# A first batch led through the weights' conversion by ties: the order of three streams on VectorE

## The chip, the cores and the metric

The kernel runs on one core of a Trainium2 chip. The metric is device time in microseconds, the median of several executions, compared with executions of the kernel before on the same chip. An execution counts as fast, or as slow where it lies over 1.5% above the fastest of the same kernel. The span of a profile is some 1.7 us shorter than the time of the same execution.

## The reference

Four batches of attention with a polynomial feature map, followed by a mixing of tokens with phases:

```python
# q, k, v: (4 batches, 4 heads, 1088 tokens, 32), S1, S2: (8, 32)
def phi(x):
    a = einsum('rd,bhsd->bhsr', S1, x)
    b = einsum('rd,bhsd->bhsr', S2, x)
    return einsum('bhsi,bhsj->bhsij', a, b).reshape(..., 64)
q_p, k_p = phi(q), phi(k)
kv  = einsum('bhsf,bhsd->bhfd', k_p, v)
num = einsum('bhsf,bhfd->bhsd', q_p, kv)
den = einsum('bhsf,bhf->bhs', q_p, k_p.sum(axis=2))[..., None] + 1e-6
x = num / den                                # to (4, 1088, 128)
theta = x @ w_theta
zr, zi = x * cos(theta), x * sin(theta)
y = einsum('ts,bsd->btd', w_tok_r, zr) + einsum('ts,bsd->btd', w_tok_i, zi)
u = x + y
out = u + maximum(u @ w_ch, 0)
```

The weights `w_tok_r` and `w_tok_i` (1088 x 1088 each) come as 64-bit floats, which the kernel turns into 32-bit ones.

## The kernel before

Three streams share VectorE (DVE) and ScalarE (ACT): the 34 pieces of weights, batch 0, and batch 1. The builder places instructions on each engine by rank; `level` sets the rank, and the ranks are, best first: first (batch 0), weights, out, attention (batches 1 to 3), mixing.

```python
def load_f32(dst, src):                     # one piece of weights, 128 x 544
    st = stg.tile([P, PIECE], I64, tag="st", ...)             # 4 buffers
    nc.sync.dma_start(st, src)
    step = stg.tile([P, PIECE, 2], I16, tag="step", bufs=2)
    A.activation(dst, ...); A.activation(step[:, :, 1] ...); A.activation(step[:, :, 0] ...)
    ts(x, x, 3, ALU.logical_shift_left)     # the two VectorE passes of a piece
    tt(V, x, x, step ..., ALU.add)

def keys_slices(b):                         # ... largest key, power of two ipk
    for h in range(H):
        A.activation(kx[:, :, h], kn[:, :, h], AF.Copy, scale=ipk[:, b, 0, h:h + 1])
    ks = work.tile([P, 3, NC * P], F16, tag="ksl", bufs=1)    # a buffer of its own
    big = work.tile([P, NC * P], F32, tag="r", bufs=1)
    # ... five VectorE passes of 128 x 1152: the keys in three f16 slices
# query_slices(b): likewise, into q0, q1, q2 of their own
# matrices(b): key sums, then a few dozen small dependent steps to the feature matrix mv[b]
# keys_values(b), features(b), denominators(b), queries(b, g): to x and z, three groups of tokens

def attention(b):
    features(b)
    denominators(b)
    for g in range(NG):
        queries(b, g)

with level("first"):
    # ... loads, S1 and S2 in tiles of their own
    query_slices(0); matrices(0); keys_values(0, spare); attention(0)
with level("attention"):
    keys(1); attention(1); keys(2)
mixing(0, True)                             # 102 matmuls: 17 rows of weights, 3 groups, 2 halves each
with level("attention"):
    attention(2); keys(3)
mixing(1, False)
# ... attention(3), mixing(2, False), mixing(3, False)
```

A mixing matmul shows in the trace as two half-matmuls, and counts below ("102") are of these: 17 rows x 3 groups x 2.

## Time and profile before

| before | |
|---|---|
| time | 358.36 us (358.15 to 359.53, 3 runs; a fourth came with the result) |
| span of the profile | 357.9 us |
| mv of batch 0 complete | 77.6 us |
| last weights pass on VectorE ends | 117.4 us |
| key slices of batch 1 complete | 120.2 us |
| mv of batch 1 complete | 154.5 us |
| first z of batch 1 (its start) | 188.8 us |

### The profile page before, as it was taken

The numbers are of one execution on the slowest core, as the hardware profiler recorded it, in microseconds if no ns is written. First come the engines' busy times: TensorE is split into PE (matmuls) and PEld (weight loads), VectorE is DVE, ScalarE is ACT, GpSimd is POOL, SyncE is SP. The second block draws the span as 40 slices with busy tenths as digits, with TensorE's granted clock in tenths as the row PEclk, the third lists the DMA queues.
The fourth block names the chain that finished last, engine by engine and source line by source line (L and its number), as shares of the span: only waits on it lengthen the run. The fifth ranks groups of instructions, "written<-read, shape, count | busy, mean of one in ns | idle before, by whom it ended". The sixth has DMA issues, their size and how long they took to land.

```text
span 357.9 us, 4021 instructions
## 1 busy us (share of the span) xinstructions
PE 274.9 (77%) x1355; PEld 192.1 (54%) x1355; DVE 250.4 (70%) x713; ACT 153.8 (43%) x313; POOL 0.7 (0%) x6
## 2 busy tenths in 40 slices
PE   0406680145327999999689999996999999999994
PEld 0304480023226676776357777674777766776562
DVE  4898886985996699559948794896589569542111
ACT  0799729997958442061134413312335131332000
POOL 0000000000000000000000000000000000000000
PEclk9999955556555899999969999997899999999998
DMA  7668447883720012020010122000000000000010
GB/s 289 214 229 269 153 145 243 293 304 108 238 59 4 2 65 69 0 67 3 22 40 2 65 66 70 21 22 20 0 0 3 0 9 15 22 20 0 0 44 18
DMA packets 11604, 28.78 MB, mean 80 GB/s; under 512 B 1216, under 2 KB 5568, under 8 KB 11584
## 3 DMA queue, kind: packets, MB, share of 16 engines
q1 hardware_dynamic: 11376, 28.51, 24.3%
q8 instruction: 10, 0.16, 0.2%
q14 instruction: 10, 0.08, 0.1%
q10 hardware_dynamic: 208, 0.02, 0.0%
HBM read 26.30 MB, written 2.23 MB: 80 GB/s over the span
## 4 chain that ended last, share of the span: by engine, by line
PE 69%; DVE 17%; ACT 8%; DMA 3%; issue 1%; ACTq 0%
PE y L566 36%; PE w L519 4%; PE acc L398 3%; ACT step L135 3%; PE w L539 2%; PE y L576 2%; PE y L398 2%; PE w L446 2%; ACT step L136 2%; DVE wT L93 2%; PE w L513 2%; PE w L388 2%; DMA s_t_st<-s_t 2%; PE acc L306 2%; PE w L447 2%; PE w L534 1%
## 5 line engine op out<-in xcount | busy, mean ns | idle before, releaser
L566 PE MATMUL y<-wT,zst 128*128 128x384 f32 (+1 forms) x384 | 134.8, 481 | 1.4 <-DVE zst L93 1.4
L566 PEld LDWEIGHTS y<-wT,zst 128*128 128x128 f32 x384 | 68.1, 193 | 30.6 <-DVE zst L93 2.3
L585 ACT COPY ot<-y 128x384 f32<-128x384 f32 (+2 forms) x16 | 6.0, 398 | 62.1 <-PE y L580 62.1
L135 ACT ACTIVATE step<-st 128x544 f16<-128x544 f32 (+1 forms) x35 | 27.8, 795 | 4.3 <-DVE wT L93 4.2
L93 DVE CUSTOM_DVE_ANT_0 wT<-wT,step 128x1088 uint16<-128x1088 uint16 x34 | 24.4, 718 | 5.8 <-ACT step L136 5.8
L519 PEld LDWEIGHTS w<-kvbd,qpT 128*128 128x128 f32 x144 | 21.6, 213 | 11.3 <-ACT qpT L517 10.4
L136 ACT ACTIVATE step<-st 128x544 int16<-128x544 uint32 (+1 forms) x35 | 27.4, 784 | 0.0
L519 PE MATMUL w<-kvbd,qpT 128*128 128x64 f32 x144 | 23.4, 297 | 3.2 <-ACT qpT L517 3.1
L134 ACT ACTIVATE wT<-st 128x544 f32<-128x544 f32 x34 | 22.9, 685 | 2.3 <-DMA st<-w_tok 2.2
L517 ACT COPY qpT<-w 128x256 f32<-128x256 f32 x36 | 12.9, 367 | 24.6 <-PE w L513 24.5
L513 PE MATMUL w<-ident,qp 128*128 128x128 f32 x72 | 14.6, 304 | 7.7 <-DVE qp L93 7.6
L93 DVE TENSOR_TENSOR uT<-xT,y 128x384 f32<-128x384 f32 (+1 forms) x12 | 6.3, 529 | 19.2 <-PE y L566 19.1
L97 DVE TENSOR_SCALAR tn<-w 128x384 f32<-128x384 f32 x12 | 6.7, 557 | 17.8 <-PE w L539 17.8
L536 ACT COPY xT<-w 128x384 f32<-128x384 f32 x12 | 5.7, 475 | 29.8 <-PE w L534 29.8
L449 ACT COPY lv<-w 128x384 f32<-128x384 f32 x36 | 14.9, 504 | 8.3 <-PE w L448 8.2
L513 PEld LDWEIGHTS w<-ident,qp 128*128 128x128 f32 x72 | 10.1, 170 | 9.8 <-ACT wT L134 8.1
L97 DVE TENSOR_SCALAR wT<-wT 128x544 int32<-128x544 int32 x34 | 14.6, 435 | 0.0
L446 PE MATMUL w<-mv,q 128*128 128x384 f16 x36 | 13.4, 372 | 0.8 <-DVE mv L93 0.8
L398 PEld LDWEIGHTS acc<-ld_v,kp 128*128 128x128 f32 x108 | 13.0, 192 | 1.5
L539 PEld LDWEIGHTS w<-w,xT 128*128 128x128 f32 x72 | 10.6, 215 | 5.2 <-ACT xT L536 4.5
L404 ACT COPY kvbd<-acc 64x64 f32<-64x64 f32 x6 | 1.2, 206 | 27.6 <-PE acc L398 27.6
L100 DVE SCALAR_TENSOR_TENSOR fl<-lv 128x864 f32<-128x864 f32 x4 | 4.2, 1054 | 12.3 <-ACT lv L449 12.3
(230 smaller groups left out, 523.5 us busy)
## 6 DMA issues: line engine op xcount, KB each, us to landing
st<-w_tok SPq DMA_DIRECT2D x34, 544.0 KB, 4.6
ld_k<-k_l SPq DMA_DIRECT2D x4, 576.0 KB, 4.0
ld_q<-q_l SPq DMA_DIRECT2D x4, 576.0 KB, 4.4
ld_v<-v_l SPq DMA_DIRECT2D x4, 576.0 KB, 3.8
out<-ot SPq DMA_DIRECT2D x8, 192.0 KB, 2.1
out<-ot SPq DMA_DIRECT2D x4, 128.0 KB, 1.8
st<-w_sq SPq DMA_DIRECT2D x1, 256.0 KB, 4.6
out<-ot SPq DMA_DIRECT2D x4, 32.0 KB, 1.8
```

The lines of the kernel that those rows point to most:

```text
L93: eng.tensor_tensor(out=o, in0=a, in1=b, op=op)
L97: V.tensor_scalar(out=o, in0=a, scalar1=s1, scalar2=s2, op0=op0, **kw)
L134: A.activation(dst, hi.bitcast(F32), AF.Copy, scale=2.0**-112)
L135: A.activation(step[:, :, 1].bitcast(F16), hi.bitcast(F32), AF.Copy, scale=2.0**-60)
L136: A.activation(step[:, :, 0], lo.bitcast(U32), AF.Copy, scale=2.0**-29)
L398: nc.tensor.matmul(kv[:, n], kp[:, i * H + 2 * n:i * H + 2 * n + 2].rearrange("p h i j -> p (h i j)"), vn[:, c, 2 * n:2 * n + 2].rearrange ...
L446: nc.tensor.matmul(lp, q0, flat[:, 0:4 * W], start=True, stop=False, skip_group_check=True)
L449: A.copy(lv[:, :, :, c].rearrange("p l t n -> p (l t) n"), lp.rearrange("p (x n) -> p x n", n=HR))
L513: nc.tensor.transpose(tr[:, n * P:(n + 1) * P], qp[:, i * H + 2 * n:i * H + 2 * n + 2].rearrange("p h i j -> p (h i j)"), ident)
L519: nc.tensor.matmul(num[:, i * P + n * 2 * D:i * P + (n + 1) * 2 * D], qpT[:, n], kvbd[b][:, n], start=True, stop=True)
L539: nc.tensor.matmul(th[:, i * P:(i + 1) * P], xT[:, i * P:(i + 1) * P], w2[:, 0], start=True, stop=True)
L566: nc.tensor.matmul(yp[:, :t1 - t0], z, wT[:, i, t0:t1], start=(i == 0), stop=(i == NK - 1))
```

## The change

The intent is to bring batch 0 to its mixing early. Its parts:

- **Ties.** The VectorE passes of each piece of weights are queued behind a chosen instruction of batch 0's chain, a few pieces per place. Seven pieces instead of 23 then lie ahead of mv(0).
- **Split.** Batch 0's features, denominators and queries go group by group (three groups of tokens).
- **Hold.** Batch 1's VectorE work is queued behind batch 0's first group.
- **Row order.** Rows of weights are loaded and mixed in the order of the groups (real and imaginary row of a chunk side by side), so mixing can start on the first group.
- **S1 and S2** in one tile of 128 x 48.
- To make room, the key and the query slices share one buffer ("sl"); batch 0's z gets a tile of its own; three step buffers instead of two.

```diff
+    order = [j * NF + i for i in range(NF) for j in range(2)] + [NK - 1]
...
-        for i in range(NK):
+        for i in order:
             for n in range(0, S, PIECE):
                 load_f32(wT[:, i, n:n + PIECE], w_tok[i][:, n:n + PIECE])   # notes both passes in `rows`
...
-        ks = work.tile([P, 3, NC * P], F16, tag="ksl", name="ksl", bufs=1)
+        ks = work.tile([P, 3, NC * P], F16, tag="sl", name="ksl", bufs=1)
...
-        sl = [work.tile([P, NC * P], F16, tag=f"q{i}", name=f"q{i}", bufs=1) for i in range(3)]
+        sl = work.tile([P, 3, NC * P], F16, tag="sl", name="qsl", bufs=1)
...
-        query_slices(0)
-        matrices(0)
-        keys_values(0, spare)
-        attention(0)
+        keys_features(0)
+        matrices(0)                      # gate(1) at three places inside
+        query_slices(0)
+        gates.extend([tiles["ready", 0]] * 3)
+        with tc.issue_after(tiles["ready", 0]):
+            for g in range(NG):
+                features(0, g * GC, (g + 1) * GC)
+                if g == 0:
+                    keys_values(0, spare)
+                denominators(0, g * GC, (g + 1) * GC)
+                gate(3)
+                mixed(0, g, numerator(0, g))
+                gate(4)
+                if g == 0:
+                    behind = last_on_dve()
+        gate(2 * NK)
+        for i, ins in enumerate(rows):   # order on VectorE alone, no wait
+            tc.add_manual_dep(ins, gates[i // 2].name, ...)
     with level("attention"):
-        keys(1)
+        with tc.issue_after(behind):
+            load(1, "kqv")
+            keys_powers(1)
+            query_powers(1)
+            keys(1)
         attention(1)
         keys(2)
```

(`gate(n)` puts the last VectorE instruction so far n times on the list of places; cut here: S1 and S2, the split of functions, buffers.)

## The prediction

> **What bounds the kernel now.** I read the busy shares and slices of the page first, then each engine's busy time in stretches cut at four events, then the chain that ended last, the costs by form, and the order of time of each engine in the first 190 us.
>
> ```profile
> PE 274.9 (77%) x1355; PEld 192.1 (54%) x1355; DVE 250.4 (70%) x713; ACT 153.8 (43%) x313; POOL 0.7 (0%) x6
> ...
> PE   0406680145327999999689999996999999999994
> ...
> DVE  4898886985996699559948794896589569542111
> ACT  0799729997958442061134413312335131332000
> ...
> PEclk9999955556555899999969999997899999999998
> ```
>
> TensorE is nearly full from the 13th slice on, but in the first 12 (to about 115 us) it is busy for less than half and from the 6th has a halved clock, while VectorE and ScalarE turn the 34 pieces of 64-bit weights into floats and carry the first batch through its small steps. The four stretches are: keys of batch 0 in until its feature matrix mv is ready (77.3); until the first mixing matmul of batch 0 (115.9); until the first of batch 1 (189.7); the rest.
>
> ```profile
> 4.80:77.30 72.50, 26.50 (x125) 20.34 (x126) 60.36 (x223) 55.95 (x98) 0.00 (x0) 0.78 0.70 237
> 77.30:115.90 38.60, 19.34 (x77) 13.75 (x76) 30.17 (x67) 30.84 (x56) 0.00 (x0) 0.54 0.38 121
> 115.90:189.70 73.80, 69.03 (x357) 47.64 (x358) 56.13 (x141) 22.05 (x51) 0.00 (x0) 0.93 0.11 33
> 189.70:357.90 168.20, 159.64 (x798) 110.29 (x796) 102.26 (x267) 44.97 (x110) 0.00 (x0) 0.97 0.07 21
> ```
>
> (After the stretch and its length: PE, PE weight load, DVE, ACT, POOL busy, clock, DMA share, GB/s.) The fourth stretch is 95% TensorE: its 168.2 us stay unless that work changes. In the third TensorE is full too, but with filler: the mixing of batch 0 is there while batch 1 creeps forward. Its chain of waits shows that the stretch ends on batch 1 and not on TensorE:
>
> ```profile
> 173.20 0.56 DVE uT L100
> ...
> 177.16 0.76 DVE r L97
> ...
> 180.62 1.22 DVE ksl L100
> ...
> 189.72 1.35 PE y L566 x4
> ```
>
> The last mixing matmuls of batch 0 end near 172.5; then VectorE carries the chain (denominators of batch 1, slices of batch 2), and TensorE can mix again at 189.7. So the time is: start of batch 1's mixing, plus 168.
>
> **What the Trainium skill says.** (1) "TensorE: Matmul & The Clock Gate", Part 1, says that the array runs at half clock until it has been busy for some 3.4 us and falls back when idle. The trace agrees: the stretch 77.3 to 115.9 was granted 0.54, the later ones 0.93 and 0.97, and four half-matmuls of the mixing take 2.92 us at 115.9 but 1.35 us at 189.7. (2) The same page, "Architectural detail", says that VectorE and ScalarE take their queue strictly first in, first out. So a weights pass that waits for ScalarE stops everything behind it; the trace has VectorE idle 2.52 us before a weights pass at 56.3, with batch 0's next small copy behind it. (3) "VectorE: DVE Perf Modes", the errata section, gives every VectorE operation a fixed cost beside its length (151 cycles for fp32 tensor_tensor). Here 128x288 takes 0.45 us and 128x1152 1.36, which fit that to 0.01 us, so an operation cut in three pays the fixed cost three times.
>
> **The change part by part.**
>
> *Weights.* The same 34 pieces, the same passes:
>
> ```profile
> L135 ACT ACTIVATE step<-st 128x544 f16<-128x544 f32 x34 | 27.3, 804 | 4.3 <-DVE wT L93 4.2
> L136 ACT ACTIVATE step<-st 128x544 int16<-128x544 uint32 x34 | 27.0, 793 | 0.0
> L93 DVE CUSTOM_DVE_ANT_0 wT<-wT,step 128x1088 uint16<-128x1088 uint16 x34 | 24.4, 718 | 5.8 <-ACT step L136 5.8
> L134 ACT ACTIVATE wT<-st 128x544 f32<-128x544 f32 x34 | 22.9, 685 | 2.3 <-DMA st<-w_tok 2.2
> L97 DVE TENSOR_SCALAR wT<-wT 128x544 int32<-128x544 int32 x34 | 14.6, 435 | 0.0
> ```
>
> Issued back to back, a piece takes 0.64+0.35 = 1.0 us on VectorE and 1.9 on ScalarE (starts at 60.87, 62.79, 64.68). What is new is their place. By the built order only 7 pieces lie before mv(0) instead of 23; 20 lie between there and the last z of batch 0, and 7 behind it.
>
> *S1 and S2 in one tile* take away some 15 VectorE instructions of 0.1 to 0.2 us each: about 2 us, on the first path. Splitting batch 0's denominators into three adds two more sets of about 24 instructions with the same elements in all: 48 fixed costs near 0.1 us, +5 us of VectorE. (The built order has 755 VectorE instructions against 715.)
>
> *Stage A, to mv(0).* I summed the start-to-start times of VectorE instructions in the new order, from the operation on the keys at 4.8 to the last writing of mv: 35.6 us, where the old stretch had 60.4. Following the waits by hand (keys' slices start near 14 instead of 18.5, the 18 key-sum matmuls run about 25.5 to 30.5, then the small cuts, 0.2 us for each dependent one, and four round trips to TensorE) adds about 11 us: mv(0) near 51, 26 us earlier.
>
> *Stage B, to the end of batch 0's mixing.* Behind that stand 58.8 us of VectorE: 27 pieces 26.6, denominators about 20, kp and qp 5.2, x, tn, tt, z 7.2. ScalarE has about 24 pieces less what three step buffers hold ready, 45 us, and 13 of batch 0: 58. Two equal loads that wait for each other do not run at 100%: at the 83% of the first old stretch (60.4 of 72.5) the 58.8 become 71, so about 122. TensorE must also do 17 mixing matmuls after the last z: 17 x 0.65 at full clock = 11 us from about 115. Both say about 122 to 126, against 115.9 for the *start* of this mixing before. The mixing (102 half-matmuls, about 33 us) is thus gone from the later path, but the front ends later.
>
> *Stage C, batch 1 to its first mixing.* The order puts batch 1's key slices behind the last weights and beside batch 0's output. VectorE has 45.3 us there; before it had 56.1 in 73.8 us (76%). At 76% this is 60 us. Followed by hand with nothing left to fill the waits (slices 8, key sums 4.5, to mv(1) 24, features 7, denominators, qp and slices of batch 2 20, x to z 7) it is about 68 to 70.
>
> *Stage D* stays 168.2.
>
> Sum by shares: 122 + 2 + 60 + 168 = 352. Sum by steps: 125 + 68 + 168 = 361. The share method lets waits be as well filled as they were, the step method puts them all end to end, which overlaps less than engines do; gates placed with this much care also suggest that someone found them useful on the chip, which favours the lower one. I take 354.
>
> **The rivals.**
>
> *1. The front is what counts, and TensorE's 33 us come off the end.* If batch 0 leaves the front by 112 (ScalarE's bare sum, 51 + 58, plus a last pass) and batch 1's small steps run fast because TensorE's queue is empty (60 us), mixing 1 starts near 172: 340. For it: TensorE was 94% busy in the third stretch, so small matmuls of batch 1 stood in a queue. Against: VectorE had 17.7 us idle there, yet the stretch is a chain of some 150 dependent VectorE steps, whose length TensorE hardly sets.
>
> *2. Batch 1 becomes bare.* What was taken off TensorE was filler, so the gap moves from 40-115 us to about 125-190, at half clock: features of a batch take 0.72 us a group at half clock (77.6, 78.3, 79.0) against 0.37 at full (157.55, 157.92). Then C is 70 or more and the time 360 to 368. For it: the order has no mixing between batch 0's end and batch 1's first z. Against: C also loses batch 0's x, tn, tt and z.
>
> *3. DMA becomes the bound.* 24 pieces of 544 KB in about 70 us are less than the 304 GB/s reached at 60 to 80 us. I hold this unlikely.
>
> **Range and chances.** Stage B may be off by 7 us either way, C by 6, A by 4, and D by 3: together about 10. The middle of the two sums less the lean gives 354, and 8 in 10 from 343 to 365. Two per cent are at 351.2 and 365.5. So 0.38 for faster, 0.50 within, 0.12 slower.
>
> **What would show it.** Right: the last piece of mv(0) near 51; the last weights pass near 122 (before 116.7); nearly all of batch 0's mixing between 76 and 126; a stretch of 60 to 68 us behind it in which TensorE is less than half busy at a low clock and VectorE's waits are for TensorE; then about 168 us as before. Wrong: weights ending before 112 (my stage B loses too much to waits); batch 1's first mixing less than 55 us behind batch 0's last (then rival 1, and TensorE's queue was what slowed batch 1); or a fourth stretch that differs from 168 by over 4 us, because mixing in the new order of rows starts better or because the later batches come apart.

## More of the kernel before

A line holds start, length, engine, source line, operation, output<-input, and in brackets the idle time before it with what ended it.

```profile
77.74 0.15 DVE L97 TENSOR_SCALAR ipk<-pw 128x4 f32<-128x4 f32 x1
...
108.14 0.44 DVE L97 TENSOR_SCALAR wT<-wT 128x544 int32<-128x544 int32 x1
108.49 0.75 DVE L97 TENSOR_SCALAR ksl<-kx 128x1152 f16<-128x1152 f32 x1
...
110.00 0.71 DVE L93 CUSTOM_DVE_ANT_0 wT<-wT,step 128x1088 uint16<-128x1088 uint16 x1
...
116.67 0.71 DVE L93 CUSTOM_DVE_ANT_0 wT<-wT,step 128x1088 uint16<-128x1088 uint16 x1
117.30 0.75 DVE L97 TENSOR_SCALAR r<-kx 128x1152 f32<-128x1152 f32 x1
118.09 0.76 DVE L97 TENSOR_SCALAR ksl<-r 128x1152 f16<-128x1152 f32 x1
118.88 1.36 DVE L100 SCALAR_TENSOR_TENSOR ksl<-kx,ksl 128x1152 f16<-128x1152 f32 x1
```

The scale of batch 1's keys (ipk) is there at 77.9. Batch 1's key slices (ksl) begin at 108.5, between passes of the weights (wT) and before batch 0's first z; they are done 3 us behind the last weights pass.

## The result, and the profile after

| | before | after |
|---|---|---|
| time, median of 4 | 358.94 us (358.15 to 359.90) | 378.11 us (376.12 to 379.49) |
| span of the profile | 357.9 | 375.4 |
| mv(0) complete | 77.6 | 54.5 |
| last weights pass ends | 117.4 | 132.0 |
| key slices of batch 1 complete | 120.2 | 139.2 |
| mv(1) complete | 154.5 | 172.0 |
| first z of batch 1 | 188.8 | 205.8 |

The changed kernel is slower: the ratio is 1.053, with a 95% interval from 1.047 to 1.059. A ratio here is the mean time of one kernel's fast runs over that of the other's of the same rounds, so not quite the ratio of the medians quoted.

The page of the changed kernel (busy times; busy tenths of 40 slices; chain that ended last):

```profile
PE 287.1 (76%) x1355; PEld 200.3 (53%) x1355; DVE 257.2 (69%) x753; ACT 155.2 (41%) x311; POOL 0.7 (0%) x6
...
PE   1655039659699967088147999998899999999994
...
PEclk9999555568989989555656999999699999999999
...
PE 58%; DVE 25%; ACT 12%; issue 2%; DMA 2%; SPq 0%; ACTq 0%; DVEq 0%
```

TensorE (PE) is busier in the first 14 slices on the whole than before, as intended. But a hole has opened in slices 15 to 22, some 132 to 206 us, with a low clock. In the chain VectorE has 25%, where the page of before has 17. Cut at the same four events as in the prediction (columns as there):

```profile
4.80:54.40 49.60, 19.64 (x85) 13.84 (x85) 40.59 (x160) 30.64 (x54) 0.00 (x0) 0.81 0.58 198
54.40:132.00 77.60, 64.00 (x259) 44.36 (x259) 61.62 (x177) 60.49 (x106) 0.00 (x0) 0.79 0.52 166
132.00:206.50 74.50, 42.48 (x208) 31.17 (x208) 50.24 (x130) 19.08 (x43) 0.00 (x0) 0.66 0.08 24
206.50:375.40 168.90, 160.60 (x805) 110.83 (x803) 103.08 (x270) 45.02 (x110) 0.00 (x0) 0.97 0.07 21
```

The fourth stretch is unchanged (168.9 for 168.2). So nearly the whole loss of 17.5 us in the span is that batch 1's first z comes 17 us later. The order of time on ScalarE and VectorE around the last weights says what stands before it:

```profile
130.50 0.79 ACT L147 ACTIVATE step<-st 128x544 int16<-128x544 uint32 x1
131.16 1.78 ACT L304 ACTIVATE kx<-ld_k,ipk 128x288 f32<-128x288 f32 x4
```

```profile
118.71 0.16 DVE L108 TENSOR_SCALAR ipk<-pw 128x4 f32<-128x4 f32 x1
...
131.31 0.72 DVE L104 CUSTOM_DVE_ANT_0 wT<-wT,step 128x1088 uint16<-128x1088 uint16 x1 [0.83 <-ACT step L147]
131.96 0.55 DVE L104 TENSOR_TENSOR uT<-xT,y 128x384 f32<-128x384 f32 x1
132.97 0.76 DVE L108 TENSOR_SCALAR ksl<-kx 128x1152 f16<-128x1152 f32 x1 [0.47 <-ACT kx L304]
...
137.82 1.35 DVE L111 SCALAR_TENSOR_TENSOR ksl<-kx,ksl 128x1152 f16<-128x1152 f32 x1
```

The scale of batch 1's keys (ipk) is there at 118.9, 41 us later than before: the hold keeps batch 1 back until batch 0's first z at 81.6, and then its first VectorE passes stand behind others of better rank. Its four scalings on ScalarE (kx) come 12 us later, behind the last of the weights' passes (step, 130.50), and the slices on VectorE behind those. Before, the slices began at 108.5. In the stretch behind it, VectorE's waits are nearly all for TensorE or for ScalarE's copies of its results (us in total, times, longest):

```profile
DVE fl L111 <- ACT lv L486: 4.2, 1, 4.2
DVE tn L108 <- PE w L583: 3.1, 1, 3.1
DVE pw L230 <- PE acc L227: 3.0, 1, 3.0
DVE cm L104 <- PE acc L327: 2.0, 1, 2.0
DVE kp L104 <- PE acc L431: 1.9, 1, 1.9
```

### The profile page after: what moved, and what is told of

Its sections match the earlier page's. It is cut to its first block, busy times and chain, and to the rows that moved or that the text cites. A ratio compares the mean times of both kernels' runs of the same rounds, so it can differ in the third digit from the quotient of the medians.

```text
span 375.4 us, 4081 instructions
## 1 busy us (share of the span) xinstructions
PE 287.1 (76%) x1355; PEld 200.3 (53%) x1355; DVE 257.2 (69%) x753; ACT 155.2 (41%) x311; POOL 0.7 (0%) x6
## 3 DMA queue, kind: packets, MB, share of 16 engines
q1 hardware_dynamic: 11584, 28.53, 23.4%
## 4 chain that ended last, share of the span: by engine, by line
PE 58%; DVE 25%; ACT 12%; issue 2%; DMA 2%; SPq 0%; ACTq 0%; DVEq 0%
PE y L610 25%; PE acc L431 4%; PE w L554 4%; ACT step L147 3%; PE w L583 3%; PE w L413 2%; ACT step L146 2%; PE y L431 2%; PE w L548 2%; ACT wT L145 2%; DVE lv L104 2%; ACT lv L486 2%; DVE qp L104 2%; PE w L483 2%; PE y L620 2%
## 5 line engine op out<-in xcount | busy, mean ns | idle before, releaser
L610 PE MATMUL y<-wT,zst 128*128 128x384 f32 (+1 forms) x288 | 100.8, 475 | 0.0
L610 PEld LDWEIGHTS y<-wT,zst 128*128 128x128 f32 x288 | 49.8, 190 | 19.3 <-issue 0.7
L610 PE MATMUL y<-wT,z 128*128 128x384 f32 (+1 forms) x120 | 45.8, 514 | 7.3 <-DVE z L104 6.0
L610 PEld LDWEIGHTS y<-wT,z 128*128 128x128 f32 x120 | 23.4, 208 | 21.3 <-DVE z L104 7.0
L145 ACT ACTIVATE wT<-st 128x544 f32<-128x544 f32 x34 | 23.4, 695 | 9.6 <-DMA st<-w_tok 9.6
L431 PEld LDWEIGHTS acc<-ld_v,kp 128*128 128x128 f32 x108 | 17.2, 238 | 2.5 <-DVE ipn L382 0.3
L483 PE MATMUL w<-mv,qsl 128*128 128x384 f16 x36 | 14.4, 400 | 5.2 <-DVE mv L104 4.2
L431 PE MATMUL acc<-ld_v,kp 128*128 128x64 f32 x108 | 16.9, 319 | 0.3 <-DVE ipn L382 0.3
L548 PEld LDWEIGHTS w<-ident,qp 128*128 128x128 f32 x72 | 10.6, 177 | 10.5 <-issue 9.7
L325 PE MATMUL acc<-ksl 128*128 128x384 f16 x27 | 9.9, 389 | 7.4 <-DVE ksl L111 7.4
L349 PE MATMUL acc<-sz,cz 128*128 128x32 f16 (+3 forms) x16 | 2.8, 182 | 16.3 <-DVE cz L108 16.3
```

Source lines behind the costliest of these rows:

```text
L145: A.activation(dst, hi.bitcast(F32), AF.Copy, scale=2.0**-112)
L431: nc.tensor.matmul(kv[:, n], kp[:, i * H + 2 * n:i * H + 2 * n + 2].rearrange("p h i j -> p (h i j)"), vn[:, c, 2 * n:2 * n + 2].rearrange ...
L483: nc.tensor.matmul(lp, q0, m[:, 0:4 * W], start=True, stop=False, skip_group_check=True)
L548: nc.tensor.transpose(tr[:, n * P:(n + 1) * P], qp[:, i * H + 2 * n:i * H + 2 * n + 2].rearrange("p h i j -> p (h i j)"), ident)
L610: nc.tensor.matmul(yp[:, :t1 - t0], z, wT[:, i, t0:t1], start=(n == 0), stop=(n == NK - 1))
```

## The experiments

Two theories stood at the start. **Queue:** ties, hold and split put batch 1's chain behind the weights, so it starts late. **Bareness:** what was taken off TensorE was filler, so batch 1's chain runs at a low clock and gets longer. A rival to both was the prediction's own: less work on TensorE in that stretch should be a gain. (In the expectations, G stands for the ties and H for the hold, the two parts of Queue; C for the clock, which is Bareness; S for the split.) Eighteen kernels were run, all of them correct but one that is wrong on purpose; each edit is against the changed kernel unless it says otherwise. One table holds what they gave (events in us, from the profiled run; the last column is the time left behind the first z of batch 1):

| run | time, us | ratio to before | last weights | key slices (1) | mv(1) | first z(1) | rest |
|---|---|---|---|---|---|---|---|
| before | 358.9 | 1 | 117.4 | 120.2 | 154.5 | 188.8 | 169.2 |
| after | 378.1 | 1.053 | 132.0 | 139.2 | 172.0 | 205.8 | 169.6 |
| no_gates | 370.4 | 1.027 | 100.7 | 130.5 | 169.1 | 201.5 | 168.2 |
| no_hold | 374.2 | 1.041 | 138.3 | 125.4 | 169.3 | 203.8 | 168.6 |
| no_gates_no_hold | 367.6 | 1.024 | 98.8 | 131.0 | 164.7 | 195.4 | 169.6 |
| filler | 371.4 | 1.031 | 132.7 | 140.2 | 169.6 | 201.9 | 168.4 |
| before_mix0_one_row | 368.4 | 1.024 | 117.4 | 121.8 | 163.9 | 198.0 | 169.9 |
| both_unsplit | 354.2 | 0.985 | 102.7 | 112.7 | 146.9 | 182.9 | 169.5 |
| both_mix_late (slow profile) | 365.8 | 1.010 | 98.7 | 128.3 | 161.3 | 197.0 | 169.8 |
| mix_late | 369.8 | 1.029 | 130.6 | 135.7 | 165.5 | 198.8 | 168.3 |
| unsplit_only | 375.8 | 1.047 | 128.5 | 135.3 | 170.1 | 204.5 | 169.6 |
| both_unsplit_mix_late | 351.1 | 0.980 | 104.1 | 114.1 | 146.6 | 182.2 | 167.1 |
| before_s_merged | 360.2 | 1.004 | 118.9 | 122.1 | 154.7 | 188.6 | 168.8 |
| unsplit_no_gates | 359.8 | 1.003 | 101.8 | 124.5 | 153.5 | 188.8 | 168.5 |
| ties_at_mv0 | 376.2 | 1.051 | 120.8 | 132.5 | 169.9 | 204.3 | 169.8 |
| unsplit_no_hold | 348.4 | 0.973 | 135.1 | 85.7 | 135.5 | 177.7 | 169.5 |
| before_row_order | 360.6 | 1.007 | 115.4 | 118.3 | 152.9 | 187.4 | 171.3 |
| before_mix_late | 362.8 | 1.014 | 117.3 | 121.7 | 158.2 | 191.8 | 169.7 |
| unsplit_keys1_first (slow profile) | 354.4 | 0.986 | 141.7 | 112.0 | 158.5 | 191.9 | 169.6 |
| keys1_first (slow profile) | 360.7 | 1.001 | 145.1 | 115.8 | 163.0 | 194.9 | 169.7 |

(A slow profile is of a run over 1.5% above that kernel's fastest; its events are then some us late, and only the ratio, which leaves such runs out, is compared.) The rest is 167 to 171 us in all of them: **the span is the first z of batch 1 plus about 169**, and the end of the weights says nothing of it. The last weights come at 98.8 in a run of 367.6 and at 135.1 in one of 348.4. The runs were made in rounds on several chips, where the kernel before took 358.0 to 359.8 us; so a difference of some 2 us between times of different rounds is not to be read, and the ratios are the better measure.

### no_gates: without the ties

```diff
-        for i, ins in enumerate(rows):
-            tc.add_manual_dep(ins, gates[i // 2].name, ...)
```

> The changed kernel without the ties of the weights' VectorE passes to chosen places; all else as changed. By the built order some 20 pieces of weights then lie ahead of mv(0) again (7 in the changed kernel), and batch 1's key slices come ahead of batch 0's last x instead of behind the last weights. Theory G (the ties made it slow: they pile weights, denominators and the groups into one stretch that ends at 132 instead of 117): mv(0) near 68, last weights pass near 118 to 122, first mixing matmul of batch 1 near 190, time 358 to 364. Rival B (bareness: whatever the order of weights, batch 1's chain has no filler and is as long): the last weights end earlier, but the chain to batch 1's first mixing stays 74 us or more behind it only where batch 1 starts late; time 368 to 378.

370.4 (one run of four slow; the fast ones mean 369.4), interval of the ratio 1.021 to 1.033: 7.7 us of the 19 come back, between the two theories. mv(0) was at 66.9, the last weights at 100.7. But batch 1's key slices still came only at 130.5, though no weights were left to stand before them: the first began at 118.43, right behind batch 0's last feature matmul (118.08), for a reason that the next run shows. The ties are one hand in the loss and not the whole.

### no_hold: without the hold

```diff
-        with tc.issue_after(behind):
+        if True:
```

> The changed kernel without the order edges that hold batch 1 behind batch 0's first group; ties of the weights stay. The built order puts batch 1's key slices among the last groups of batch 0 instead of behind the last weights. Theory H (holding batch 1 made stage C long): stage C, from the last weights pass to batch 1's first mixing matmul, falls from 74.5 to about 62, the last weights move from 132 to about 139, time 371 to 374. Theory G (the ties): 376 to 380, since the same VectorE work only changes places.

374.2, ratio 1.038 to 1.043: 4 us, at the upper edge of theory H. The lines below (ScalarE, then TensorE, then VectorE) show why so little:

```profile
60.08 0.54 ACT L304 ACTIVATE kx<-ld_k,ipk 128x288 f32<-128x288 f32 x1
```

```profile
103.56 0.25 PE L485 MATMUL w<-mv,qsl 128*128 128x192 f16 x1
```

```profile
103.84 0.76 DVE L108 TENSOR_SCALAR ksl<-kx 128x1152 f16<-128x1152 f32 x1 [0.52 <-PE w L485]
...
117.53 0.70 DVE L108 TENSOR_SCALAR ksl<-r 128x1152 f16<-128x1152 f32 x1
124.09 1.35 DVE L111 SCALAR_TENSOR_TENSOR ksl<-kx,ksl 128x1152 f16<-128x1152 f32 x1
```

The scaled keys are ready at 60.6, yet the first slice is taken at 103.8, when TensorE's L485 has ended. That is batch 0's last feature matmul, in the third group: it reads the query slices, and these share the buffer "sl" with the key slices. So the slices wait 43 us with their input ready; in one piece (unsplit_no_hold below) batch 0 is done with the buffer at 64.5, and they wait 8. Batch 1's slices nevertheless begin 5 us before those of the kernel before, and are spread over 22 us; from their end to mv(1) it takes 44 us where it took 34, while the weights go on beside them to 138.3. So an early start alone is not enough. VectorE sits idle for only 0.52 us before it, because the builder had put other work in front; so a list of waits doesn't show this dependence at its size.

### no_gates_no_hold: both away

The two edits above together.

> The changed kernel without ties and without the hold of batch 1; what stays is the split of batch 0 into groups, S1 and S2 in one tile, the order of rows. If ties and hold together are the whole loss, this is 352 to 359 (the before time less some us for S1 and S2). If the split of batch 0 into three groups and the early mixing are the loss themselves, 368 to 378.

367.6, just under the second range. Ties and hold together are 10.5 of the 19 us. The scaled keys are ready at 103.5, and again the first slice follows batch 0's last feature matmul:

```profile
118.60 0.25 PE L485 MATMUL w<-mv,qsl 128*128 128x192 f16 x1
```

```profile
118.96 0.76 DVE L108 TENSOR_SCALAR ksl<-kx 128x1152 f16<-128x1152 f32 x1 [0.59 <-ACT tn L589]
```

### filler: useless matmuls in the hole

```diff
     mixing(0, True)
+    with level("mixing"):
+        mix_sums(0, range(NG), [psum(ps_y, "y") for _ in range(NG)])
```

> The changed kernel with batch 0's 102 mixing matmuls issued a second time, into PSUM that nobody reads, at the lowest priority: the built order puts them where TensorE stood idle in stage C (from the last weights to batch 1's first mixing), and leaves VectorE's order as it was. It adds 33 us of TensorE at full clock and does nothing useful. Theory C (half clock: with nothing to do TensorE drops to half clock and every round trip of batch 1's chain grows): clock in stage C over 0.85, the 24 kv matmuls go from 8.0 to about 4 us, the features from 7.4 to about 4, stage C falls from 74.5 to 64 to 68, time 367 to 372. Rival B (the chain of dependent VectorE steps sets stage C, TensorE's clock hardly): 375 to 380. Rival Q (small matmuls of batch 1 queue behind mixing matmuls): slower, 380 to 390.

The kernel does 102 half-matmuls more, to no use, and is **6.7 us faster**: 371.4, ratio 1.026 to 1.035, in the range of theory C. VectorE's order hardly differs. First the changed kernel, then the filler run: the stretch 150 to 189, and the 36 kv matmuls of batch 1.

```profile
150.00:189.00 39.00, 19.31 (x86) 14.92 (x86) 23.75 (x84) 6.87 (x16) 0.00 (x0) 0.57 0.07 25
```

```profile
150.00:189.00 39.00, 37.47 (x184) 24.99 (x183) 29.06 (x91) 7.20 (x19) 0.00 (x0) 1.00 0.08 28
```

```profile
L431 PE MATMUL acc<-ld_v,kp 128*128 128x64 f32 x36 | 8.0, 420 | 0.3 <-DVE ipn L382 0.3
```

```profile
L431 PE MATMUL acc<-ld_v,kp 128*128 128x64 f32 x36 | 4.2, 272 | 0.0
```

The clock goes from 0.57 to 1.00, the kv matmuls from 8.0 to 4.2 us, and the stretch from the last weights to batch 1's first mixing from 74.5 to 69.8, less than the 64 to 68 expected. So bareness costs some 5 us of the 19 here, and is not the whole either.

### before_mix0_one_row: useful filler taken away

On the kernel before, batch 0 mixes one row of weights instead of 17; batch 0's output is wrong.

```diff
-        for i in range(NK):
+        for i in (range(NK) if b else (NK - 1,)):
-                nc.tensor.matmul(..., start=(i == 0), stop=(i == NK - 1))
+                nc.tensor.matmul(..., start=(i == (0 if b else NK - 1)), stop=(i == NK - 1))
```

> The kernel before with the mixing of batch 0 cut from 17 rows of weights to one (96 of 102 half-matmuls gone; batch 0's output is wrong on purpose). Theory C (what TensorE does in that stretch is filler, and keeps its clock up): 31 us of TensorE go, the clock between 132 and 189 falls from near 1.0 to 0.5 to 0.6, and the time does not fall: 357 to 364. The prediction's rival 1 (TensorE's 33 us come off the end): 325 to 345. Theory between (the chain of VectorE sets it, clock of no account): 354 to 358.

With 96 half-matmuls less, some 31 us of TensorE, the kernel before gets **9 us slower**: 368.4, ratio 1.021 to 1.027, beyond even the range of theory C. First the kernel before, then this run, from 132 to 189:

```profile
132.00:189.00 57.00, 52.23 (x263) 35.32 (x263) 43.57 (x114) 15.35 (x38) 0.00 (x0) 0.94 0.14 42
```

```profile
132.00:189.00 57.00, 32.09 (x147) 23.57 (x146) 41.30 (x117) 11.78 (x29) 0.00 (x0) 0.64 0.12 40
```

This rules out the prediction's rival 1: TensorE is 92% busy there and was not the bound. Not all of the 9 us need be the clock, since batch 0's outputs also move forward on VectorE in this run.

### both_unsplit: without ties, hold and split

```diff
-            for g in range(NG):
-                features(0, g * GC, (g + 1) * GC)
-                if g == 0:
-                    keys_values(0, spare)
-                denominators(0, g * GC, (g + 1) * GC)
-                gate(3)
+            features(0, 0, NC)
+            keys_values(0, spare)
+            denominators(0, 0, NC)
+            gate(9)
+            for g in range(NG):
```

(against no_gates_no_hold)

> As no_gates_no_hold (367.6), with batch 0's features and denominators in one piece again instead of three by group. Theory S (the split costs 48 fixed costs of VectorE, and lets the mixing of batch 0 end before batch 1 needs a filler): z of batch 0 ends near 132 instead of 138, batch 1's first z comes near 188 instead of 195, time 357 to 361. Rival (the remaining loss lies in the new order of batch 1's keys and of the slices, or in the order of rows): 365 to 369.

354.2, ratio 0.983 to 0.988, under the range: the split alone cost 13.4 us here. The expectation had the direction but put it down to 48 fixed costs and the filler; the key slices of batch 1, which begin at 103.2 instead of 118.96 and are done at 112.7 instead of 131.0, point to the shared buffer: batch 0's last feature matmul is now at 76.1, and no longer stands just before them.

### both_mix_late and mix_late: batch 0's mixing held back

```diff
+        late = next(i for i in reversed(nc.cur_bb.bb.instructions) if i.engine == mybir.EngineType.PE)
...
-    mixing(0, True)
+    with tc.issue_after(late):
+        mixing(0, True)
```

(`late`: batch 0's last theta matmul.) On no_gates_no_hold:

> As no_gates_no_hold (367.6), with batch 0's mixing queued on TensorE behind batch 0's last theta matmul; VectorE's instructions as there but for the outputs of batch 0. Theory C (the early mixing takes away the filler of batch 1's chain): clock over 0.9 from 160 to 189 instead of 0.5 to 0.7, the 24 kv matmuls and the features half as long, time 361 to 365. Rival S (it is VectorE's added work alone): 366 to 369.

365.8 with two of four runs slow; the fast ones give 1.010 (1.004 to 1.015) for the 1.024 of no_gates_no_hold. The direction is that of theory C, the size unsure. On the changed kernel:

> The changed kernel, ties and hold kept, with batch 0's mixing queued on TensorE behind batch 0's last theta matmul, so that it starts near 117 instead of 81. Theory C with Q (early mixing stands before batch 0's small matmuls, and is missed later): last weights pass near 128 instead of 132, clock over 0.9 to 170, time 366 to 371, like the filler run but with no added work. Rival (stage B is VectorE's and ScalarE's, and C the VectorE chain): weights end 131 to 133, time 374 to 379.

369.8, ratio 1.026 to 1.032: 8.3 us better than the changed kernel, in the range of theory C. But the weights ended at 130.6, hardly earlier, so the early mixing had not been in the way of batch 0 (part Q is not borne out). That it was missed later fits the clock from 132 to 172 (1.00 for 0.70), but batch 1's key slices were also done 3.5 us earlier, of the 7.0 us by which its first z is: about half of the gain can't be the clock of the hole.

### unsplit_only: ties and hold kept

The edit of both_unsplit on the changed kernel, nothing else.

> The changed kernel with ties and hold kept and only batch 0's features and denominators in one piece again (nine pieces of weights then tied behind the one set of denominators, four behind each group's z). If the split is a loss of its own that adds to that of the ties (it was 13 us without them): 363 to 367, and batch 0's last z comes 8 to 11 us earlier than 123, unless the weights hold it. If the ties had hidden the split's waits behind weights passes, the split costs only its fixed costs here: 371 to 375.

375.8, ratio 1.043 to 1.052: a little above both ranges: the split is worth 2 us here, which the two intervals do not tell from nothing, and 13 without ties and hold. Batch 0's last z comes at 109.6 instead of 123.2, and it doesn't help: batch 1's scalings wait on ScalarE behind the last weights again, though their scale is there at 106.8.

```profile
126.98 0.79 ACT L147 ACTIVATE step<-st 128x544 int16<-128x544 uint32 x1
127.64 1.78 ACT L304 ACTIVATE kx<-ld_k,ipk 128x288 f32<-128x288 f32 x4
```

### both_unsplit_mix_late, unsplit_no_gates

The first is both_unsplit with the edit of mix_late, the second unsplit_only with the edit of no_gates.

> As both_unsplit (354.2), with batch 0's mixing queued behind batch 0's last theta matmul, near 122 instead of 109, so that it reaches further into batch 1's chain. If the clock of 0.80 between 172 and 189 is worth something: clock over 0.9 there, 351 to 353. If the chain of VectorE sets it by now: 353.5 to 356.

351.1, ratio 0.974 to 0.986, in the range of the clock theory, and the clock from 172 to 189 was 0.90 for 0.80. But the interval touches that of both_unsplit (0.983 to 0.988), and batch 1's first z is only 0.7 us earlier; the rest of the 3 us lies behind it. That the clock before the first z gave them is not shown.

> The changed kernel with batch 0 in one piece and without ties, the hold of batch 1 kept. With both_unsplit (354.2) it shows what the hold costs once the split is gone: by no_gates less no_gates_no_hold 3 us, so 356 to 359; if the hold only mattered beside the split, 353 to 355; and with unsplit_only it shows what the ties cost then: 8 us by no_gates.

359.8, ratio 0.999 to 1.007, just above the range: the hold costs 5.5 us here, and the ties 16 (unsplit_only).

### before_s_merged and before_row_order: two parts alone, on the kernel before

```diff
-        load(0, "kqv")
-        st_hi, st_lo = load_pair(s_t ..., 2 * R, "s_t", copies=4)
-        s2_hi, s2_lo = load_pair(s_2, D, "s_2")
+        load(0, "k")
+        s_hi, s_lo = load_pair([... four copies of s_t ...] + [(s_2, slice(0, R), slice(n, n + D))], n + D)
+        load(0, "qv")
```

> The kernel before with S1 and S2 side by side in one tile and loaded behind the keys on the same queue; nothing else. By the prediction's step some 15 short VectorE instructions, 2 us on the first path: 355 to 358. Rival (the first path is filled with weights passes, and what is taken from it comes back there): 358 to 361.

360.2, ratio 1.000 to 1.008. mv(0) is 2 us earlier (75.5), just as the prediction's step had it, but the first z of batch 1 stays where it was (188.6): the rival.

> The kernel before with the rows of weights loaded and mixed in the new order, nothing else. Its 34 pieces are ready at 117 whatever their order, and batch 0's mixing starts there: 357 to 360. If the order lets the mixing of batches 1 to 3 start on rows that are there sooner: 353 to 356.

360.6, ratio 1.005 to 1.010, just above both ranges. The edit is the first hunk of the change above, with the same order in the mixing. The first z of batch 1 is 1.3 us earlier, and the rest is 2 us longer; why was not looked into.

### ties_at_mv0: no ties behind batch 0's groups

```diff
+        at = gates.index(tiles["ready", 0])
+        gates[at:] = [tiles["ready", 0]] * len(gates[at:])
```

> The changed kernel with the first ten pieces of weights tied as they are, and all the others tied only behind the last writing of mv(0), not behind the denominators and the z of each group; split and hold kept. The built order has the same 7 pieces ahead of mv(0), but none behind the last z. Theory late (what costs is the last seven pieces behind batch 0, ahead of batch 1's keys): last weights near 118, batch 1's first z near 199 to 202, time 368 to 372, as without ties. Theory early (what costs is the 16 pieces kept out of the first 54 us): last weights near 122 to 128, the work only changes places, time 374 to 379.

376.2, ratio 1.048 to 1.054. The weights end at 120.8, 11 us earlier, and the time is the same: so it isn't the last seven pieces. The scale of batch 1's keys was there only at 124.4, and the slices began at 127.3, behind batch 0's last z: with hold and low rank batch 1 is late even where no weights stand between its scale and its scalings.

### unsplit_no_hold: ties kept, hold and split away

The edits of both_unsplit and no_hold on the changed kernel.

> The changed kernel with its ties, batch 0 in one piece, and batch 1 not held. With unsplit_only (375.8), unsplit_no_gates (359.8) and both_unsplit (354.2) it closes the square of ties and hold. If ties cost because batch 1 stands behind them, freeing batch 1 gives much back: 358 to 364. If they cost because the weights themselves end late and mixing with them: 368 to 373.

**348.4**, ratio 0.969 to 0.977, far below both ranges, and faster than either kernel. Batch 1's key slices on VectorE:

```profile
68.50 0.75 DVE L108 TENSOR_SCALAR ksl<-kx 128x1152 f16<-128x1152 f32 x1
...
84.43 1.29 DVE L111 SCALAR_TENSOR_TENSOR ksl<-kx,ksl 128x1152 f16<-128x1152 f32 x1
```

They are done at 85.7, and mv(1) at 135.5, with the last weights pass. ScalarE is full from 105 to 132 (27.00 of 27 us): batch 1's chain of small steps now lies beside the weights, as batch 0's did. TensorE's clock from 132 to 189 was 0.79 here and 0.94 in the kernel before, so the gain doesn't come from the clock. The eight corners (median us):

| | split | in one piece |
|---|---|---|
| ties and hold | 378.1 | 375.8 |
| ties alone | 374.2 | **348.4** |
| hold alone | 370.4 | 359.8 |
| neither | 367.6 | 354.2 |

The ties gain 5.8 us in the one corner where nothing keeps batch 1 back, and cost 7 to 16 in the other three (by the ratios a gain of 4.4 us, and costs of 6 to 16).

### before_mix_late

The edit of mix_late on the kernel before, whose mixing of batch 0 starts at 115.9.

> The kernel before with batch 0's mixing queued on TensorE behind batch 0's last theta matmul (near 129 instead of 116), nothing else. Theory C (a filler is worth most where it lies beside batch 1's chain): clock over 0.9 from 172 to 189 instead of 0.8, time 355 to 358. If the lateness helps only beside the other changes: 358 to 361.

362.8, ratio 1.011 to 1.017: outside both ranges. The clock from 132 to 189 was 0.94 as before, but from 105 to 132 it fell to 0.60, and mv(1) came 3.7 us later. Later is not better as such.

### unsplit_keys1_first and keys1_first: only the rank of batch 1's keys

```diff
-    with level("attention"):
+    with level("first"):
         with tc.issue_after(behind):
             load(1, "kqv")
             keys_powers(1)
             query_powers(1)
             keys(1)
+    with level("attention"):
         attention(1)
         keys(2)
```

> As unsplit_only (375.8: ties and hold kept, batch 0 in one piece), with batch 1's key part at the rank of batch 0's work, so that the built order puts it among the weights and not behind them. If the place behind the weights is the loss: batch 1's key slices end before 115 instead of at 135, its mv before 160 instead of 170, time 352 to 362. If the hold itself is: 367 to 376.

354.4 over five runs; the three fast ones (352.95, 353.01, 354.43) give 0.986 (0.983 to 0.990). Ties and hold are as in unsplit_only, and 22 us are gone.

> The changed kernel (378.1) with ties, hold and split kept, and batch 1's key part at the rank of batch 0's work. If the place behind the weights is the loss here too: key slices end near 115 instead of 139, first z of batch 1 near 195, time 362 to 369. If the split stands in the way (the query slices of batch 0 share a buffer with the key slices of batch 1, and its last group of features comes late), or the weights and the mixing of batch 0 only move behind: 372 to 378.

360.7, of which the three fast runs (356.05, 360.23, 361.15) give 1.001 (0.994 to 1.008), below the lower range. **The changed kernel with nothing altered but the rank of batch 1's keys takes the time of the kernel before.** Its profile, though of a slow run, shows the order: the scale is there at 95.4, the first scaling follows at once on ScalarE, and VectorE takes the first slice at 101.14, as soon as the shared buffer is free (the last feature matmul starts at 100.59).

```profile
95.38 0.54 ACT L304 ACTIVATE kx<-ld_k,ipk 128x288 f32<-128x288 f32 x1 [2.51 <-DVE ipk L108]
```

```profile
101.14 0.75 DVE L108 TENSOR_SCALAR ksl<-kx 128x1152 f16<-128x1152 f32 x1
```

Its last weights come at 145.1, later than in any other run, at no cost.

## Why the prediction was wrong, point by point

**Where the time is set: right.** "The time is: start of batch 1's mixing, plus 168" held in all runs (167 to 171 behind the first z). The sum by shares, 352, fell short of the measured span, 375.4, by 23.4 us: 3.4 in stage A, 6.6 in B, 12.5 in C, 0.9 in D.

**Stage A: right in size, 3.4 us late** (the stretch was cut at 54.4, for 51). S1 and S2 gave their 2 us on the first path and nothing at the end, which the step had not asked.

**Stage B: work and share were both a little off.** VectorE was to have 58.8 us from mv(0) to the end of the weights and to be 83% busy; it had 61.62 in 77.6 us, 79%, and the stage ended at 132.0 for 122 to 126.

**Stage C: the step that failed most.** "At 76% this is 60 us": VectorE was busy for 50.2 us and not 45.3, at 67% and not 76%, so it took 74.5. The same sum by hand (68 to 70, though its terms add to 70.5) was short by 4.5 to 6.5, and the filler run shows that the low clock is worth about that (4.7 us). It also answers the prediction's remark that TensorE hardly sets the length of this chain. Why the 76% was not reached is argued, not shown: before, the mixing and batch 0's last steps lay beside the chain, and batch 1's slices among the weights, and an average share need not hold in a stretch from which exactly the other work was taken.

**The lean: wrong.** The two sums were 352 and 361, the span measured 375.4; the prediction took 354, 2.5 below their middle and 7 below the sum by steps, which was the nearer one, because the gates' placement looked tried. That is no view of the profile.

**The cause was seen and not weighed.** The prediction says that "the order puts batch 1's key slices behind the last weights", but never sets this beside the kernel before, where they began at 108.5, among the weights. The chain from there to the first z took 188.8 - 108.5 = 80 us before and 205.8 - 133.0 = 73 after: it got shorter and began 24.5 us later. That the place of batch 1's key part among the weights is the cause, the rank alone shows: 378.1 against a mean of 359.1 of the fast runs of keys1_first, all of the loss. The rank moves that whole part, from the scale to mv(1) and the kv matmuls, so the runs do not separate its late start from its slow course: over all runs it takes 68 to 109 us from the first slice to the first z. The traces say what held the start: with the hold and the weights' better rank the scale comes 41 us later than before, and the scalings wait 12 us more on ScalarE behind weights; without the hold but with the split, the shared buffer keeps the first slice to 103.8. Taking away one of hold and split gave 4 or 2 us, and both gave 30.

**The signs.** Of the signs of being wrong that the prediction named, none came: the weights ended at 132.0 (not before 112), the mixings lay over 55 us apart, the fourth stretch was 168.9. They all looked for a kernel faster than foretold, or for a change in the last stage, and none for a front that ends late.

**Rivals.** Rival 2 (bareness) was right in kind: a stretch at a clock of 0.66 from 132 to 206. At 360 to 368 it was too mild, and its part of the loss is some 5 us. Rival 1 is refuted (before_mix0_one_row). Rival 3: DMA was busy 0.52 of stage B, not the bound.

**Open.** How the 9 us of before_mix0_one_row and the 5 of the filler divide between the clock and a changed order on VectorE; why the late mixing hurts on the kernel before (4 us) and not on both_unsplit; and what the shared buffer alone costs, since no run has key and query slices in buffers of their own together with the split.

## What to carry to other kernels

When several streams share an in-order engine, ask for each what keeps it from starting: its rank, its order edges and its buffers, and find the stream whose first step sets the end. Bringing one stream forward by edges pays only if the next one may run beside it; here the same ties were worth +5.8 us or -16 us, depending on two other lines. And don't count matmuls beside a chain of small dependent steps as a cost: look at what they do for the clock. The clock isn't the aim either: the fastest run here had a lower one in that stretch (0.79) than the kernel before (0.94).

## What the Trainium skill lacked or had wrong

- "TensorE: Matmul & The Clock Gate", section "HAM oscillation — how this bites in real kernels", has idle gaps behind DMA waits and cures them by restructuring the loop or padding M. The traces agree on the effect (clock 0.57 in the hole, 1.00 with the filler). It lacks that independent matmuls put into the gap can pay off even if useless (here the gap is behind a chain on VectorE, and padding M is the page's nearest to it): 102 half-matmuls took the changed kernel from 378.1 to 371.4 us, and taking 96 useful ones from the kernel before made it 368.4 instead of 359.5, though VectorE's order moved there too.
- "Perfetto Trace Analysis", section "Optimization Strategy", advises interleaving regimes with different most-contended engines. The runs agree: with batch 1's chain beside the weights, 375.8 became 348.4. It says that consistent bubbles can mean too few buffers. It lacks that a shared buffer may show no bubble: in no_hold it kept a step back for 43 us and the trace shows 0.52 us of idle time.
- No page of it treats the rank by which instructions of several streams are placed on one in-order engine; changing it for one stream was worth 19 us (378.1 to a mean of 359.1) and 22 us (375.8 to 353.5) here.
